# The first batch's key loads issued by ScalarE instead of SyncE

## The chip, the cores and the metric

One core of a Trainium2 chip runs the whole program in one launch. The metric is the device time of one execution in microseconds (us). It is the median of several runs, and lower is better. Every time below comes from the kernel's measured runs or from one profiled execution of it. The engines are called by the names that the profile gives them: PE (TensorE, matrix multiply), DVE (VectorE), ACT (ScalarE), POOL (GpSimd) and SP (SyncE, which only issues loads and stores here).

## The reference

Two stages follow each other. The first is attention of eight heads over a sequence of 576, for eight batches; the first four heads see a local window of 32 positions, the other four every 32nd position. The second is a mixture of four experts, each a causal attention on the first stage's output, of which two are taken for each token.

```python
def _attn_ref(q, k, v):                 # q, k, v: (8, 8, 576, 64)
    scores = scale * np.matmul(q, k.transpose(0, 1, 3, 2))
    ...
    mask_local = (rel >= 0) & (rel < stride)                  # stride = 32
    mask_strided = (rel >= 0) & (pos[None, :] % stride == pos[:, None] % stride)
    masks = np.stack([mask_local if h < H // 2 else mask_strided for h in range(H)], axis=0)
    ...
    return np.matmul(attn, v).astype(np.float32)

def _moe_ref(x, w_gate, wq, wk, wv, wo):
    ...
    for e in range(E):
        q = x @ wq[e]
        k = x @ wk[e]
        v = x @ wv[e]
        scores = scale * (q @ k.transpose(0, 2, 1))
        ...
        ye = a @ v @ wo[e]
        ...
            out += mask[..., None] * w[:, :, kk:kk + 1] * ye
```

## The kernel before

**Stages.** `stage1(b, hp)` does the first attention for one batch and one pair of heads; pairs 0 and 1 are local, pairs 2 and 3 strided. The second stage (`project`, `values2`, `attend`, `out_tile`) takes over when the four pairs of a batch are done. This case is about the opening, in which the four pairs of batch 0 are loaded, transposed and scored.

**What sets the order.** Every step is recorded by `op` (line 264) and issued by `schedule` (line 293) in the order of a hand-set list of numbers, `ORDER`. That one list gives the order on every engine: an instruction stands in its engine's queue where its step stands in the list, and each engine works through its queue in order. `FILL` puts matrix multiplies of no use (line 303, "fillers" below) ahead of some steps on PE.

**Batch 0's loads.** For a local pair, `load_qk` loads queries and keys with one DMA each, 288 KB (line 500, buffers `p_160` and `p_161` for pairs 0 and 1). For a strided pair it takes three DMAs each, of 18 rows of SBUF, 288 KB in all (line 505). Pair 2 goes to the buffer `nat_168` and pair 3 to `nat_172`; they are called **A** and **B** below. The value loads are at line 551, and the first loads of batch 1 at line 500 (`nat_176`).

**Counters.** The built program gives each load one of eight counters, `DMAHW0` to `DMAHW7`, in turn along the order in which it places the loads. A load that is to use a counter again is not issued before the earlier load on that counter has landed. The wait stands in the queue of the engine that issues the load.

**What follows a load.** For a local pair PE transposes the tiles (lines 573 and 586), ACT and DVE copy the results out of PSUM to `qkt` (line 340), and PE computes the scores from `qkt` (line 630). For a strided pair PE transposes `nat` (line 602), ACT and DVE copy (line 340) and PE scores (line 644). `qkt_180` serves pairs 0 and 2, `qkt_182` pairs 1 and 3.

Of the kernel before, what the change touches and what calls it, by code (L numbers as in the profile page):

```python
# [20 lines left out]
def attention_moe_kernel(  # L21
# [20 lines left out]
    nc = tc.nc  # L42
    B, H, S, D = q.shape
# [5 lines left out]
    NJ = S // STR  # L49
# [313 lines left out]
    for j in range(4):  # L363
        r = slice(32 * j, 32 * j + 32)
# [97 lines left out]
    def stage1(b, hp):  # L462
        batch[0] = b
        h0 = 2 * hp
# [4 lines left out]
        nat = (P2[3] if b == 0 and local else NAT).new(f"nat_{n}")  # L469
# [8 lines left out]
        def pair(x):  # L478
            return nat.t[:, x] if b == 0 else nat.t[:, x * S:(x + 1) * S]
# [10 lines left out]
        def raw(x):  # L490
            return nat.t[:, x * S:(x + 1) * S]

        def load_qk(src, x, h, y):
            base = src[b, h0 + h]
            if quad:
                p_ = 64 * h + 32 * y
                nc.sync.dma_start(raw(x)[p_:p_ + 32].rearrange("p (g d) -> p g d", d=32),
                                  base.rearrange("(g t) d -> t g d", t=32)[:, :, 32 * y:32 * y + 32])
            elif local:
                nc.sync.dma_start(pair(x), src[b, h0:h0 + 2].rearrange("h (p g) d -> (h p) (g d)", g=9))  # L500
            else:
                for r in range(3):
                    n_ = (11 if r < 2 else 10) * D
                    p_ = 64 * x + NJ * r
                    nc.sync.dma_start(nat.t[p_:p_ + NJ, :22 * D].rearrange("p (h c) -> p h c", h=2)[:, :, :n_], strips(base, 11 * r, n_))

        def strips(base, g0, n_):
            return bass.AP(tensor=base.tensor, offset=base.offset + g0 * D, ap=[[STR * D, NJ], [S * D, 2], [1, n_]])

        dm = [(0.51, 0.48)] if quad else [(0.44, 1.15)] if local else [(0.34, 0.67)] * 3  # L510
        for x, src in enumerate((q, k)):
            for h, y in ((0, 0), (0, 1), (1, 0), (1, 1)) if quad else ((0, 0),):
                op(*(("load_qk", {"SP": 0.54}, k0 - 30) if b > 1 else ("load_0", {"SP": 0.54}, first("x", b, hp))),
                   lambda e, src=src, x=x, h=h, y=y: load_qk(src, x, h, y), w=[nat[x]] if quad else [nat], dmas=dm)
# [8 lines left out]
        if quad:  # L523
            for x in range(2):
                op("tq", {"DVE": 0.66 if local else 1.11}, k0 - 13, lambda e, x=x: nc.vector.transpose(  # L525
                    turned(qkt.t, x), raw(x) if local else raw(x).rearrange("p (g d) -> p g d", d=32)),
                   r=[nat[x]], w=[qkt[x]])
            if not local:
                op("tq_out", {"ACT": 0.7, "POOL": 0.7}, k0 - 12, lambda e: (nc.scalar.copy if e == "ACT" else nc.gpsimd.tensor_copy)(
                    nat.t[:, :33 * NJ].rearrange("p (g r j) -> p g r j", g=11, r=3), thirds(qkt.t, 0)),  # L530
                   r=[qkt[0]], w=[nat[0], nat[1]])
# [29 lines left out]
        if local and not quad:  # L561
# [6 lines left out]
            for x in range(2):  # L568
# [7 lines left out]
                for a in range(2):  # L576
                    for h in range(2):
# [3 lines left out]
                           r=[tp], w=[qkt[0], qkt[1]])  # L581
# [7 lines left out]
            for h in range(2):  # L589
# [3 lines left out]
                   r=[tp], w=[qkt[0], qkt[1]])  # L593
# [25 lines left out]
        p = (PL if local else PSR).new(f"p1_{n}")  # L619
# [37 lines left out]
        for h in range(2):  # L657
            op("mask", {"DVE": dve(N // 2)}, k0 - 10, lambda e, h=h: nc.vector.tensor_tensor(
                pv()[:, h], sp[h].t[:, :ni * nk].rearrange("p (i c) -> p i c", c=nk), msk, ALU.add),
               r=[sp[h]], w=[p[h]])  # L660
# [23 lines left out]
        for step in range(6):  # L684
            for h_ in ((0, 2),) if step == 4 else groups:
                n_ = (h_[1] - h_[0]) * ni * nk
# [10 lines left out]
        if local:  # L697
            op("ptl", {"DVE": 0.73}, k0 - 2, lambda e: nc.vector.transpose(ptt.t[:, :640], p.t.rearrange("p h i c -> p (h i c)")),
               r=[p[0], p[1]], w=[ptt])
# [74 lines left out]
        for x, f_ in zip((xh, xl), XL4[b // 2]):  # L774
            c = slice(64 * (b % 2), 64 * (b % 2) + 64)
            op("xf", {"ACT": act(64), "POOL": 0.27}, k0 + 1.5, lambda e, x=x, f_=f_, c=c: (
                nc.scalar.copy if e == "ACT" else nc.gpsimd.tensor_copy)(f_.t[:, hp, c], f(x.t[:, S - 64:])),
               r=[x[3]] if local else [x[i] for i in range(3)], w=[f_[hp, b % 2]])
# [417 lines left out]
```

## Time and profile before

| | |
|---|---|
| Time, median of 3 runs | 443.27 us (443.09 to 443.4) |
| Profiled execution, its own time | 443.52 us |
| Its span (first to last instruction) | 441.8 us |
| PE busy in the span | 432.2 us, 98% |
| DVE, ACT, POOL busy | 360.0 (81%), 262.5 (59%), 218.5 us (49%) |
| DMA queues of loads and stores | one, SP's: 40.67 MB, 41.7% of 16 engines' time |

A row of the timeline gives the start in us from the span's start, the duration, the engine, the line, what is written and read, and the number of instructions merged in it. In brackets stands the idle time before it and what ended that. `SPq` is the queue in which SP issues DMAs: such a row is the issue, not the transfer.

### The profile page before, as it was taken

The page shows a single profiled execution, that of the slowest core. Times are in us where ns is not written, and L with a number is a line of the kernel's source. Part 1 is how long each engine was busy: PE and PEld are TensorE (multiplying, and loading weights), DVE is VectorE, ACT ScalarE, POOL GpSimd, SP SyncE. Part 2 cuts the span into 40 slices and gives each one's busy share as a digit, 9 for nine tenths or more (in the row PEclk, how much of TensorE's full clock was granted, in tenths as well). Part 3 has the DMA queues.
Part 4 walks back from the last instruction along what each step waited for, and adds up shares of the span by engine and source line. Part 5 has one row for each costly group of instructions (what it writes and reads, how often), then busy time and mean ns, then how long its engine had stood idle before and what let it go on. Part 6 is the DMA issues. An engine that isn't in the chain of part 4 may idle for free.

```text
span 441.8 us, 19136 instructions
## 1 busy us (share of the span) xinstructions
PE 432.2 (98%) x7762; PEld 384.8 (87%) x7762; DVE 360.0 (81%) x1133; ACT 262.5 (59%) x823; POOL 218.5 (49%) x404
## 2 busy tenths in 40 slices
PE   8999999999999999999999999999999999999996
PEld 8887998979799989989889888998789888988874
DVE  5798999999998999798898778788977985447761
ACT  2584635886656565647557555568684666354661
POOL 4263850786736445377336442747607472219430
PEclk9999999999999999999999999999999999999999
DMA  6666646656554635273446344074432120011013
GB/s 176 170 168 155 124 99 115 123 108 117 87 98 107 129 78 86 63 149 76 113 95 130 64 118 119 1 130 92 96 85 68 55 75 6 1 49 50 26 72 120
DMA packets 156272, 41.89 MB, mean 95 GB/s; under 512 B 145976, under 2 KB 149432, under 8 KB 156184
## 3 DMA queue, kind: packets, MB, share of 16 engines
q1 hardware_dynamic: 156184, 40.67, 41.7%
q8 instruction: 61, 1.00, 1.0%
q14 instruction: 27, 0.22, 0.2%
HBM read 31.20 MB, written 9.44 MB: 92 GB/s over the span
## 4 chain that ended last, share of the span: by engine, by line
PE 86%; DVE 9%; SPq 1%; DMA 1%; issue 1%; ACT 1%; POOL 0%; DVEq 0%; POOLq 0%; ACTq 0%
PE bank L908 20%; PE bank L1112 11%; PE bank L1083 11%; PE bank L855 9%; PE bank L994 7%; PE bank L1050 6%; PE bank L974 3%; PE bank L644 3%; PE bank L738 3%; PE bank L630 2%; PE bank L757 2%; PE bank L303 2%; DVE p L1001 1%; PE bank L818 1%; PE bank L920 1%; PE bank L708 1%
## 5 line engine op out<-in xcount | busy, mean ns | idle before, releaser
L1031 POOL TENSOR_SCALAR p<-p,st,wt 128x256 f32<-128x256 f32 (+3 forms) x128 | 77.2, 616 | 40.3 <-DVE st L1015 34.8
L1006 ACT ACTIVATE p<-p,st 128x512 f32<-128x512 f32 (+3 forms) x128 | 72.0, 568 | 9.1 <-DVE st L1001 9.0
L1001 DVE CUSTOM_DVE_ANT_0 p<-bank,m_cau 128x384 f32<-128x384 f32 (+3 forms) x128 | 58.8, 483 | 8.9 <-PE bank L994 7.5
L340 ACT COPY th<-bank 128x384 f32<-128x384 f32 (+2 forms) x106 | 41.8, 434 | 16.7 <-PE bank L1050 13.9
L525 DVE STREAM_TRANSPOSE qkt<-nat 128x576 f32<-128x576 f32 x48 | 47.6, 1004 | 1.7 <-DMA nat<-in_q_dram 1.2
L1083 PE MATMUL bank<-th,vs 128*64 128x192 f32 (+4 forms) x512 | 48.4, 337 | 0.1
L720 ACT CAST xh<-bank 128x160 fp32r<-128x160 f32 (+4 forms) x112 | 29.1, 320 | 29.1 <-PE bank L738 16.2
L929 ACT CAST qk<-bank 128x288 fp32r<-128x288 f32 x64 | 24.7, 400 | 35.9 <-PE bank L908 34.5
L1083 PEld LDWEIGHTS bank<-th,vs 128*64 128x64 f32 x512 | 33.7, 137 | 13.4 <-issue 6.2
L722 DVE TENSOR_TENSOR xl<-bank,xh 128x160 fp32r<-128x160 f32 (+4 forms) x112 | 32.2, 321 | 6.5 <-ACT xh L720 6.3
L855 PE MATMUL bank<-wh_v,xh 128*128 128x260 f32 x128 | 36.7, 287 | 0.0
L855 PE MATMUL bank<-wh_v,xl 128*128 128x260 f32 x128 | 36.2, 283 | 0.0
L855 PE MATMUL bank<-wl_v,xh 128*128 128x260 f32 x128 | 36.1, 282 | 0.0
L908 PE MATMUL bank<-xh,wh_q 128*128 128x288 f32 x120 | 35.8, 298 | 0.0
L908 PE MATMUL bank<-xh,wh_k 128*128 128x288 f32 x120 | 35.8, 298 | 0.0
L908 PE MATMUL bank<-xl,wh_q 128*128 128x288 f32 x120 | 35.4, 295 | 0.0
L908 PE MATMUL bank<-xl,wh_k 128*128 128x288 f32 x120 | 35.4, 295 | 0.0
L908 PE MATMUL bank<-xh,wl_q 128*128 128x288 f32 x120 | 35.3, 294 | 0.0
L908 PE MATMUL bank<-xh,wl_k 128*128 128x288 f32 x120 | 35.3, 294 | 0.0
L1050 PEld LDWEIGHTS bank<-ident,p 64*128 64x128 f32 x800 | 30.3, 139 | 4.7 <-issue 1.9
L1050 PE MATMUL bank<-ident,p 64*128 64x64 f32 x800 | 34.3, 226 | 0.0
L931 DVE TENSOR_TENSOR qkl<-bank,qk 128x288 fp32r<-128x288 f32 x64 | 27.6, 444 | 8.2 <-ACT qk L929 8.2
(183 smaller groups left out, 1269.2 us busy)
## 6 DMA issues: line engine op xcount, KB each, us to landing
out_dram<-ys SPq DMA_DIRECT2D x32, 256.0 KB
nat<-in_q_dram SPq DMA_DIRECT2D x96, 72.0 KB
nat<-in_k_dram SPq DMA_DIRECT2D x96, 72.0 KB
v<-in_v_dram SPq DMA_DIRECT2D x96, 40.0 KB
v<-in_v_dram SPq DMA_DIRECT2D x48, 54.0 KB
v<-in_v_dram SPq DMA_DIRECT2D x32, 48.0 KB
v<-in_v_dram SPq DMA_DIRECT2D x32, 45.0 KB
out_dram<-ys SPq DMA_DIRECT2D x8, 128.0 KB
```

Of the source, the lines that this page charges most:

```text
L340: (nc.scalar.copy if e == "ACT" else nc.vector.tensor_copy)(dst, src)
L525: op("tq", {"DVE": 0.66 if local else 1.11}, k0 - 13, lambda e, x=x: nc.vector.transpose(turned(qkt.t, x), raw(x) if local else raw(x).rea ...
L722: op("xl", {"DVE": dve(n_)}, key + 0.5, lambda e, s_=s_, x_=x_: nc.vector.tensor_sub(x_(xl.t), s_(xa.t), x_(f(xh.t))), r=[xa, xh[u]], w=[x ...
L855: nc.tensor.matmul(vp.t[:, :NV], xx.t[:, t0:t0 + 128], ww.t[:, kt, :], start=i == 0, stop=i == 11)
L908: nc.tensor.matmul(pj.t[:, :HS], ww.t[:, kt, ep * 128:(ep + 1) * 128], xx.t[:, c], start=i == 0, stop=i == 11)
L994: nc.tensor.matmul(sp[a].t[:, :nk], x.t[r, 0, q0:q0 + 128], y.t[r, 1, :nk], start=i == 0, stop=i == 2)
L1001: lambda e, sp=sp, p=p, a=a, nk=nk, ci=ci: nc.vector.tensor_tensor_reduce(out=p.t[:, a, :nk], in0=sp[a].t[:, :nk], in1=m_cau[:, S - nk:], ...
L1006: op("exp2", {"ACT": 0.285 + 0.00084 * nk}, k_ + 1, lambda e, p=p, a=a, ci=ci, nk=nk: nc.scalar.activation(p.t[:, a, :nk], p.t[:, a, :nk], ...
L1031: lambda e, p=p, a=a, ci=ci, t=t, nk=nk: nc.gpsimd.tensor_scalar(p.t[:, a, :nk], p.t[:, a, :nk], st.t[:, 20 + ci + a:21 + ci + a], wt.t[:, ...
L1050: nc.tensor.transpose(tp[hf].t[:, 64 * c:64 * c + 64], src, ident[r, r])
L1083: nc.tensor.matmul(acc.t[o, c0:c0 + cn], vw, th[a].t[:, s0:s0 + cn], start=j == 0, stop=j == idx[-1], skip_group_check=True)
L1112: nc.tensor.matmul(yp.t[:, :DM], xx.t[:, c0:c0 + 128], ww.t[:, ep, :], start=i == 0, stop=i == 5)
```

## The change

One line is added to `load_qk`, and two of its three loads use it: for batch 0 and the keys (`x` is 1) they are issued from ACT's queue (`nc.scalar`), else from SP's as before. The third form, `quad`, is for batches from 2 on and is not touched.

```diff
         def load_qk(src, x, h, y):
             base = src[b, h0 + h]
+            dma = nc.scalar if b == 0 and x else nc.sync
             if quad:
...
             elif local:
-                nc.sync.dma_start(pair(x), src[b, h0:h0 + 2].rearrange("h (p g) d -> (h p) (g d)", g=9))
+                dma.dma_start(pair(x), src[b, h0:h0 + 2].rearrange("h (p g) d -> (h p) (g d)", g=9))
             else:
                 for r in range(3):
...
-                    nc.sync.dma_start(nat.t[p_:p_ + NJ, :22 * D].rearrange("p (h c) -> p h c", h=2)[:, :, :n_], strips(base, 11 * r, n_))
+                    dma.dma_start(nat.t[p_:p_ + NJ, :22 * D].rearrange("p (h c) -> p h c", h=2)[:, :, :n_], strips(base, 11 * r, n_))
```

Eight DMAs change their queue: one for each local pair and three for each strided pair. `ORDER` is the same. The following lists show two queues near the start; after each row stand the semaphores it waits for (`PE_49`, `DVE_49` and the like are the engines' own, the `DMAHW` ones the loads' counters). Line numbers after the change are one higher.

ACT before, its first instructions: the copies out of the transposes of pairs 0 (`qkt_180`) and 1 (`qkt_182`).

```order
L340 ACT_TABLE_LOAD
L340 COPY qkt_180<-bank_66 64x128 [waits PE_49]
L340 COPY qkt_180<-bank_65 64x64x4 [waits DVE_49]
L340 COPY qkt_180<-bank_67 64x64x4 [waits DVE_49,PE_49]
L340 COPY qkt_180<-bank_65 64x64x4
L340 COPY qkt_180<-bank_67 64x64x4
L340 COPY qkt_182<-bank_69 64x64x4 [waits PE_49]
L340 COPY qkt_182<-bank_68 64x64x4 [waits DVE_49]
```

ACT after, from its first copy on; the two local key loads (`p_160` and `p_161`) stand ahead of the table load.

```order
L340 COPY qkt_180<-bank_66 64x128 [waits PE_49]
L340 COPY qkt_180<-bank_65 64x64x4 [waits DVE_49]
L340 COPY qkt_180<-bank_67 64x64x4 [waits DVE_49,PE_49]
L340 COPY qkt_180<-bank_65 64x64x4
L506 DMA nat_168<-in_k_dram 18x2x704 [waits DMAHW5_49]
L506 DMA nat_168<-in_k_dram 18x2x704 [waits DMAHW6_49]
L506 DMA nat_168<-in_k_dram 18x2x640 [waits DMAHW7_49]
L340 COPY qkt_180<-bank_67 64x64x4
L506 DMA nat_172<-in_k_dram 18x2x704 [waits DMAHW0_49]
L506 DMA nat_172<-in_k_dram 18x2x704 [waits DMAHW1_49]
L506 DMA nat_172<-in_k_dram 18x2x640 [waits DMAHW2_49]
L340 COPY qkt_182<-bank_69 64x64x4 [waits PE_49]
```

A's three key loads stand between the fourth and the fifth copy of pair 0, and B's behind the fifth. In the built program A's wait for the second landing on counters 5, 6 and 7, and B's for the third on counters 0, 1 and 2.

SP before, from A's loads on (ahead of them: the four local loads, on counters 0 to 3, and the gate's weights, on 4).

```order
L505 DMA nat_168<-in_k_dram 18x2x704 [waits DVE_49]
L505 DMA nat_168<-in_k_dram 18x2x704
L505 DMA nat_168<-in_k_dram 18x2x640
L505 DMA nat_168<-in_q_dram 18x2x704 [waits DMAHW0_49]
L505 DMA nat_168<-in_q_dram 18x2x704 [waits DMAHW1_49]
L505 DMA nat_168<-in_q_dram 18x2x640 [waits DMAHW2_49]
L505 DMA nat_172<-in_q_dram 18x2x704 [waits DMAHW3_49,DVE_49]
L505 DMA nat_172<-in_q_dram 18x2x704 [waits DMAHW4_49]
L505 DMA nat_172<-in_q_dram 18x2x640 [waits DMAHW5_49]
L505 DMA nat_172<-in_k_dram 18x2x704 [waits DMAHW6_49]
L505 DMA nat_172<-in_k_dram 18x2x704 [waits DMAHW7_49]
L505 DMA nat_172<-in_k_dram 18x2x640 [waits DMAHW0_49]
```

SP after, from A's loads on (ahead of them: the two local query loads, on counters 1 and 3, and the gate's weights, on 4).

```order
L506 DMA nat_168<-in_q_dram 18x2x704 [waits DVE_49]
L506 DMA nat_168<-in_q_dram 18x2x704
L506 DMA nat_168<-in_q_dram 18x2x640
L506 DMA nat_172<-in_q_dram 18x2x704 [waits DMAHW0_49,DVE_49]
L506 DMA nat_172<-in_q_dram 18x2x704 [waits DMAHW1_49]
L506 DMA nat_172<-in_q_dram 18x2x640 [waits DMAHW2_49]
L552 DMA v_184<-in_v_dram 32x5x64 [waits DMAHW3_49]
L552 DMA v_184<-in_v_dram 32x5x64 [waits DMAHW4_49]
L552 DMA v_184<-in_v_dram 32x6x64 [waits DMAHW5_49]
L552 DMA v_184<-in_v_dram 32x5x64 [waits DMAHW6_49]
L501 DMA nat_176<-in_q_dram 128x576 [waits DMAHW7_49]
L501 DMA nat_176<-in_k_dram 128x576 [waits DMAHW0_49,DVE_49]
```

A's queries stand where A's keys stood, with the first use of counters 5, 6 and 7. Their second use is by the third and fourth value load and by the queries of batch 1, which before stood behind all strided loads. On PE, DVE and POOL no row moves.

## Rows read from the trace of the kernel before

**Rows 1.** The page: busy us of each engine (share of the span), number of instructions.

```profile
PE 432.2 (98%) x7762; PEld 384.8 (87%) x7762; DVE 360.0 (81%) x1133; ACT 262.5 (59%) x823; POOL 218.5 (49%) x404
```

**Rows 2.** Stretches: from:to, length, busy us as in rows 1, clock, DMA share, GB/s.

```profile
5.30:11.60 6.30, 6.30 (x53) 6.08 (x52) 2.94 (x16) 2.48 (x6) 0.85 (x4) 1.00 0.61 140
...
20.60:45.00 24.40, 22.94 (x709) 20.18 (x709) 22.28 (x59) 15.18 (x45) 12.02 (x16) 1.00 0.66 158
45.00:437.00 392.00, 389.17 (x6705) 346.88 (x6704) 324.40 (x1010) 237.96 (x760) 200.36 (x363) 1.00 0.40 86
```

**Rows 3.** Waits of PE, first 60 us: who <- for whom, us in total, times, longest.

```profile
PE bank L303 <- POOL ident masks.py:199: 1.4, 1, 1.4
PE bank L602 <- DVE xl L722: 0.7, 1, 0.7
```

**Rows 4.** Timeline of SP's queue of issues, opening; start us, duration us.

```profile
3.14 1.12 SPq L505 DMA_DIRECT2D nat<-in_k_dram  x3
...
8.77 0.27 SPq L505 DMA_DIRECT2D nat<-in_q_dram  x1
9.19 0.27 SPq L505 DMA_DIRECT2D nat<-in_k_dram  x1
9.79 0.27 SPq L505 DMA_DIRECT2D nat<-in_k_dram  x1
10.77 0.27 SPq L505 DMA_DIRECT2D nat<-in_k_dram  x1
11.81 0.32 SPq L551 DMA_DIRECT2D v<-in_v_dram  x1
...
12.96 1.20 SPq L551 DMA_DIRECT2D v<-in_v_dram  x1
14.21 0.44 SPq L551 DMA_DIRECT2D v<-in_v_dram  x1
```

**Rows 5.** Waits of SP's queue, first 16 us.

```profile
SPq L505 <- DMA nat<-in_k_dram: 0.8, 2, 0.5
```

**Rows 6.** Timeline of ACT, opening.

```profile
8.43 0.83 ACT L340 COPY qkt<-bank 64x128 f32<-64x128 f32 x2 [6.35 <-PE bank L586]
...
10.69 0.42 ACT L340 COPY qkt<-bank 64x256 f32<-64x256 f32 x1
11.13 0.42 ACT L340 COPY qkt<-bank 64x256 f32<-64x256 f32 x1
11.99 1.58 ACT L340 COPY qkt<-bank 64x256 f32<-64x256 f32 x4 [0.44 <-DVE qkt L340]
14.84 0.76 ACT L340 COPY qkt<-bank 128x324 f32<-128x324 f32 x2 [1.26 <-PE bank L602]
```

**Rows 7.** Timeline of PE, opening; line 303 is the fillers.

```profile
10.88 0.83 PE L303 MATMUL bank<-ident 128*128 128x128 f32 x6
11.64 1.04 PE L630 MATMUL bank<-qkt 64*32 64x64 f32 x80
12.61 1.60 PE L303 MATMUL bank<-ident 128*128 128x128 f32 x12
14.14 0.95 PE L602 MATMUL bank<-ident,nat 54*128 54x54 f32 x24
...
15.86 0.92 PE L644 MATMUL bank<-qkt 64*64 64x54 f32 x48
```

**Rows 8.** DMA issues of the first 60 us: number of them, KB each.

```profile
v<-in_v_dram SPq DMA_DIRECT2D x24, 40.0 KB
...
nat<-in_q_dram SPq DMA_DIRECT2D x2, 288.0 KB
```

**Rows 9.** Table of stretches again: the last column is what the DMA moved, GB/s.

```profile
7.50:12.00 4.50, 4.50 (x75) 4.38 (x75) 2.96 (x7) 2.48 (x7) 0.00 (x0) 1.00 0.60 142
...
15.60:20.00 4.40, 4.27 (x141) 3.75 (x142) 3.90 (x10) 2.30 (x6) 0.72 (x1) 1.00 0.87 241
```

**Rows 10.** Timeline of PE, its first instructions.

```profile
1.42 1.65 PE L303 MATMUL bank<-ident 128*128 128x128 f32 x6 [1.42 <-POOL ident masks.py:199]
```

## Prediction

> **What bounds the kernel now.** The first view is the page's busy line: TensorE (PE) is busy for 432.2 of 441.8 us [rows 1]. The second is the table of stretches: PE is busy for all 6.30 us from 5.3 to 11.6, for 22.94 of 24.40 us from 20.6 to 45, and for 389.17 of 392 us after that [rows 2]. The third is PE's own waits in the first 60 us: 1.4 us at the very start for the identity matrix, 0.7 us once for VectorE, and no load at all [rows 3]. So a load that comes earlier frees nothing on PE, and whatever holds PE in the opening moves everything behind it.
>
> The opening is then read engine by engine. On SP's queue, the issue times also tell landings, since an issue that waits for a counter starts when the load on it lands: A's three key loads go out from 3.14, and SP's issues at 8.77, 9.19 and 9.79 are the ones that wait for them [rows 4]; the wait view has two of SP's waits as ended by landing keys [rows 5]. On ScalarE (ACT), the last copy of the first pair's transposed keys and queries starts at 10.69 and takes 0.42; the copies of the second pair follow at 11.13 and 11.99, and those of A's transposes at 14.84 [rows 6]. On PE, fillers start at 10.88, the first scores at 11.64, twelve fillers at 12.61, A's transposes at 14.14 and A's scores at 15.86 [rows 7]. The first scores need ACT's copy of 10.69, which ends at 11.11: 0.53 us before PE gets there. That is the only cover PE has against a late ACT.
>
> **What the change removes and adds.** SP loses eight issues. Their price is small (1.12 us for the three from 3.14 on, 0.27 each for those around 9 [rows 4]), and since PE waits for no load the gain is nothing. The two local key loads move to the head of ACT's queue, where ACT has nothing to do before 8.43 but load a table [rows 6]; they cost nothing, since the table load is done long before that.
>
> The six strided key loads are the matter. In ACT's instructions they stand where the written order has them, between the copies: A's three after the fourth copy, before the one of 10.69, and B's three right behind it. And each waits: A's for the second landing on counters 5, 6 and 7, B's for the third on counters 0, 1 and 2. I work out when these come.
>
> SP's queue now has A's queries where A's keys were, so they land when the keys did, at 8.77, 9.19 and 9.79, and B's queries where A's queries were: 10.77, 11.81 and about 12.0 [rows 4]. The second users of counters 5, 6 and 7 are the third and fourth value load and the queries of batch 1. The third value load can go out at 8.77 and takes 1.20 us to issue, the next 0.44, if they take what they took at 12.96 and 14.21 [rows 4]; so the queries of batch 1 go out near 10.5. They land behind B's queries (12.0), four value loads (some 40 KB each, 164,000 bytes) and their own 288 KB (295,000 bytes) [rows 8]. The DMA moved 241 GB/s in a stretch of such loads and 142 in one of strided loads [rows 9], so the value loads take 0.7 us and the queries 1.2: they land at **13.9**. The bounds: if everything from 9.79 on, B's queries too (295,000 bytes, 754,000 in all), went at 241, it would be 12.9; if at 142, 15.1.
>
> So A's last key load is issued at 13.9 instead of before 4.26. It takes about 0.35 (no row of before has ACT issue a load; the nearest are SP's, 0.27 to 0.44), the held copy 0.42 and its signal a few hundredths: the first scores start at 14.75, not 11.64. **First term: +3.1 us** (bounds +2.1 and +4.3).
>
> Next, B's keys wait for the other load of batch 1 and two value loads, which land 1.2 and twice 0.2 us behind the 13.9: 15.5. ACT has issued the last one at 15.8, makes the five copies of the second pair (0.42 each [rows 6]) by 17.9, and is then due for A's transposes, which on PE's moved schedule end at about 18.2. So this second hold is covered by 0.3 us; if the first cover were gone it would cost what it lacks, up to a microsecond where B's keys come late.
>
> A's keys themselves must be there when PE reaches A's transposes, 14.14 + 3.1 = 17.25. Issued at 13.9, they share the DMA with the other load of batch 1 and four value loads (295,000 and 164,000 bytes, 1.9 us at 241) and need 2.1 us of their own at 142: 17.9 if they go last, 16 if the two queues take turns from the start. I take the middle of nothing and 0.6. **Second term: +0.3 us** (0 to +0.6, and to +1.6 with the second hold uncovered).
>
> What goes back later: PE's idle time from 20.6 to 45 is 1.46 us [rows 2], and the one long wait in it is for VectorE [rows 3], whose work comes from PE's and ACT's and moves along. I take nothing, with -1.2 as the bound. SP's own later loads wait for PE's progress and have run ahead by then, so they add nothing. Sum: **+3.4 us**, bounds about +1 and +6.
>
> [...] The trace shows the opening's loads limited by what the DMA moves: three strided loads of 288 KB in all issued within 1.2 us land 5 to 6 us later [rows 4]. [...]
>
> **The rivals.** *The held issue does not hold the copies.* Were a waiting load to let later copies pass, the first scores would be on time, and only A's transposes would wait for keys landing at 16 to 17.9 instead of being due at 14.14: +1.9 to +3.8, 445.2 to 447.1 us. Against it: on SP the loads behind a waiting one stay behind it, up to 1.0 us between 9.79 and 10.77 [rows 4]. Chance 0.04.
>
> *PE's clock falls.* PE would stand idle for about 3 us, which it never does in this trace after 1.4. [...] Chance 0.13; it decides if the first scores come later than my 14.75 rather than sooner.
>
> *Faster.* SP is free of eight issues, its loads of batch 1 go out up to 4 us earlier, and VectorE's chain behind them gets ahead: at most the 1.2 us of waits PE has there, 442.1 us. It decides only if the counters that ACT waits for are filled before the copy of 10.69 is due, that is if batch 1's queries land by then, 3 us before my estimate and at the time they are issued. Chance 0.03.
>
> *Nothing happens.* The hold stays within PE's 0.53 us of cover: 443.3 us. It needs those queries by 10.9. The same rows speak against it. Chance 0.04.
>
> **How the numbers follow.** The profiled execution took 443.52 us around its span of 441.8, 0.25 above the median of three, 443.27. 443.52 + 3.4 = 446.9; against the median, which later runs are compared with, **446.7 us**. Forecast (+1.3 to +4.9): 0.76. Range for 8 in 10: from 444.8, the low bound of the first term with a little given back, to 449.0, which takes in the clock's case. A difference under 0.2% (0.9 us) can't be told from none here. Faster 0.03, the same 0.05 (the case of nothing and the edge of the forecast), slower 0.92.
>
> **What would show it.** In the profile after: ACT's copy of 10.69 near 14.3, with idle time before it that a DMA ends; three loads of nat from in_k issued by ACT near 13 to 14 and three more to about 15.8; PE's first scores near 14.75 with idle time before them, released by ACT; A's transposes at about 17.5, and from there to the end a constant shift. SP's loads of batch 1 go out near 10.5 instead of behind the issue at 14.21. If the first scores stand within 0.5 us of 11.64, my reading of ACT's queue is wrong; if they stand near 14.75 and the end moves by much less, PE had time to give back that I have not seen; if fillers show 1.6 us per dozen more, the clock fell.

## The result and the profile after

The changed kernel takes **447.45 us** (median of 4 runs, 446.57 to 450.92) against 443.18 for the kernel before beside it. The ratio is 1.011, 95% interval 1.0072 to 1.0148: 3.2 to 6.6 us slower. Six later runs gave 448.3 us, ratio 1.0112 (1.0083 to 1.0141). Two single executions that took far longer than all others (795.17 us of the kernel before, 658.96 of one experiment) are left out of the ratios. The profiled execution is the slowest of the first four: 450.92 us around a span of 449.2, with a mean granted clock of 0.989; the other three had 0.995 to 0.998. So its opening is read for what happens where, and the medians for what it costs.

PE's busy line of the page, which answers to [rows 1]: 5.5 us more for the same number of instructions.

```profile
PE 437.7 (97%) x7762; PEld 389.2 (87%) x7762; DVE 359.5 (80%) x1133; ACT 262.1 (58%) x823; POOL 217.7 (48%) x404
```

The table of stretches (as [rows 2]; the last three columns are granted clock, DMA share, GB/s). The clock is below 1.00 from 11.6 to 45 (0.79 and 0.87 on the mean) and 1.00 again behind. About 4.7 of PE's 5.5 us lie in the products from 16.25 to 27.1, which took 12.1 us by their rows, against 7.4 for the same ones before; the column falls to 0.50 there.

```profile
11.60:20.60 9.00, 6.18 (x124) 5.33 (x123) 2.49 (x7) 2.80 (x8) 0.72 (x1) 0.79 0.62 156
20.60:45.00 24.40, 23.62 (x655) 20.90 (x657) 20.41 (x54) 15.31 (x42) 10.75 (x15) 0.87 0.47 122
45.00:437.00 392.00, 389.24 (x6887) 347.13 (x6884) 327.90 (x1020) 238.42 (x763) 201.60 (x365) 1.00 0.41 87
```

Cut finer, one microsecond each, the same trace shows 1.00 still while PE stands idle, and 0.50 from 17, shortly after it works again, to about 27.

```profile
14.00:15.00 1.00, 0.00 (x0) 0.00 (x0) 0.00 (x0) 0.16 (x1) 0.00 (x0) 1.00 0.71 160
...
17.00:18.00 1.00, 1.00 (x6) 1.00 (x6) 0.45 (x1) 0.99 (x3) 0.40 (x1) 0.50 0.62 132
...
26.00:27.00 1.00, 1.00 (x6) 0.86 (x5) 1.00 (x4) 0.40 (x2) 0.00 (x0) 0.50 0.00 0
```

PE's waits in the first 60 us (as [rows 3]): a new one, for ACT, at the first scores.

```profile
PE bank L631 <- ACT qkt L340: 2.7, 1, 2.7
```

ACT's timeline (as [rows 6]; `ACTq` rows are ACT's issues of loads). The fourth copy ends at 11.33, then nothing until pair 2's keys (A) go out at 13.53; the held copy runs at 14.84; pair 3's keys (B) and the five copies of the second pair follow, and then ACT waits for PE.

```profile
10.47 0.86 ACT L340 COPY qkt<-bank 64x256 f32<-64x256 f32 x2 [0.56 <-DVE qkt L340]
13.53 1.27 ACTq L506 DMA_DIRECT2D nat<-in_k_dram  x3
14.84 0.41 ACT L340 COPY qkt<-bank 64x256 f32<-64x256 f32 x1 [3.51 <-DMA nat<-in_k_dram]
15.45 1.03 ACTq L506 DMA_DIRECT2D nat<-in_k_dram  x3
16.52 1.99 ACT L340 COPY qkt<-bank 64x256 f32<-64x256 f32 x5 [1.27 <-PE bank L631]
20.00 0.43 ACT L340 COPY qkt<-bank 128x324 f32<-128x324 f32 x1 [1.49 <-PE bank L603]
```

The chain of waits through that place names the load that ACT waited for first: a value load, issued on SP, which landed at 13.51. Behind it come the three issues of A's keys, the held copy and, at 15.30, the scores.

```profile
9.00 4.51 DMA v<-in_v_dram
...
13.53 0.58 ACTq L506
...
14.15 0.28 ACTq L506
...
14.47 0.33 ACTq L506
...
14.84 0.42 ACT qkt L340
...
15.30 1.02 PE bank L631 x63
```

PE's timeline (as [rows 7]): two score products go out at 12.29, since they need only the earlier copies; the other 78 wait until 15.30. The twelve fillers behind them took 2.41 us instead of 1.60, A's transposes start at 18.60 instead of 14.14, and A's scores take 1.54 instead of 0.92.

```profile
12.29 0.30 PE L631 MATMUL bank<-qkt 64*32 64x64 f32 x2
15.30 1.02 PE L631 MATMUL bank<-qkt 64*32 64x64 f32 x78 [2.72 <-ACT qkt L340]
16.25 2.41 PE L303 MATMUL bank<-ident 128*128 128x128 f32 x12
18.60 1.95 PE L603 MATMUL bank<-ident,nat 54*128 54x54 f32 x24
...
21.63 1.54 PE L645 MATMUL bank<-qkt 64*64 64x54 f32 x48
...
27.60 1.04 PE L631 MATMUL bank<-qkt 64*32 64x64 f32 x80
```

SP's queue (as [rows 4]): the first loads of batch 1 go out at 10.73, four microseconds sooner than the 14.69 of before, which frees nothing on PE.

```profile
8.05 2.10 SPq L552 DMA_DIRECT2D v<-in_v_dram  x4
10.73 0.35 SPq L501 DMA_DIRECT2D nat<-in_q_dram  x1
```

### The profile page after: what moved, and what is told of

It reads as the page before. It is cut to its first block, busy times and chain, and to the rows that moved or that the text cites. A ratio compares the mean times of both kernels' runs of the same rounds, so it can differ in the third digit from the quotient of the medians.

```text
span 449.2 us, 19136 instructions
## 1 busy us (share of the span) xinstructions
PE 437.7 (97%) x7762; PEld 389.2 (87%) x7762; DVE 359.5 (80%) x1133; ACT 262.1 (58%) x823; POOL 217.7 (48%) x404
## 4 chain that ended last, share of the span: by engine, by line
PE 82%; DVE 8%; DMA 4%; SPq 3%; issue 1%; ACT 1%; ACTq 0%; DVEq 0%
PE bank L909 20%; PE bank L1113 10%; PE bank L1084 10%; PE bank L856 9%; PE bank L995 7%; PE bank L1051 6%; PE bank L975 3%; PE bank L739 3%; PE bank L645 3%; PE bank L631 2%; DMA v<-in_v_dram 2%; SPq L498 2%; PE bank L758 2%; PE bank L303 2%; PE bank L819 1%; DMA nat<-in_q_dram 1%
## 5 line engine op out<-in xcount | busy, mean ns | idle before, releaser
L340 ACT COPY th<-bank 128x384 f32<-128x384 f32 (+2 forms) x106 | 41.8, 436 | 16.5 <-PE bank L1051 13.9
```

The lines of the kernel that those rows point to most:

```text
L340: (nc.scalar.copy if e == "ACT" else nc.vector.tensor_copy)(dst, src)
```

## The experiments

The theory after the result: the loss is ACT, held ahead of a copy that PE needs, then A's keys, which are issued late, and then the lower clock (0.50) that follows PE's idle time. The rivals: the second queue costs by itself (transfers that share the DMA), or the clock has no part in it. The microseconds behind a ratio are its distance from 1 times 443.2.

**The hold without a load.** The kernel before with copies of no use on ACT at the place in question.

```diff
         def load_qk(src, x, h, y):
+            if b == 0 and hp == 2 and x:
+                for _ in range(6):
+                    nc.scalar.copy(idle, m_cau[:, :512])
```

> The kernel before with all loads on SP, and six copies of a constant (128x512) on ACT between its fourth and fifth copy, where the change put the three key loads of pair 2. They should take some 0.6 us each, so hold ACT about 3.6 us. Theory (the loss is ACT held ahead of that copy, and PE's clock falling in the idle time): first scores at 14.5 to 15.3 instead of 11.64, a stretch at the lower clock behind them, and a time of 446.3 to 449, like the changed kernel's 447.45. Rival 1 (the loss is in the transfers: two queues share the DMA, or keys land late): no load has moved, so 443.3 to 444. Rival 2 (the hold alone, the clock falls by chance): 446.3 with the granted clock at 1.000.

Measured: 447.05 us, ratio 1.0087 (1.0072 to 1.0102), +3.9 us. ACT's timeline shows the hold, PE's the wait:

```profile
11.78 3.88 ACT L497 COPY idle<-m_cau 128x512 f32<-128x512 f32 x6
15.67 2.44 ACT L340 COPY qkt<-bank 64x256 f32<-64x256 f32 x6
```

```profile
16.13 1.02 PE L634 MATMUL bank<-qkt 64*32 64x64 f32 x78 [3.12 <-ACT qkt L340]
17.08 2.38 PE L303 MATMUL bank<-ident 128*128 128x128 f32 x12
```

The scores came later than expected (16.13 instead of 14.5 to 15.3), since PE's own start-up took a microsecond longer in this execution; the wait is the one foreseen. No load moved, and most of the loss is there, lower clock included (0.71 in the stretch from 15.6 to 20.6, 0.994 to 0.996 on the mean in all five runs). The transfers are not needed to explain that part.

**Half the hold.** The same with `range(3)`.

> The kernel before with three instead of six copies of a constant on ACT at the same place: six held ACT for 3.9 us, so three should hold it for 1.9, and PE idle for some 1.4. Theory (the hold less its cover is what PE loses, and the clock falls only in the longer idle time): 444.4 to 445.0, the clock at 1.000 in the opening. Rival (the loss is in proportion to the hold, cover or not): half of the 3.85 us that six copies cost, 445.1 and more. Rival (any idle time of PE brings the lower clock): 445.5 or more with a stretch at 0.5.

Measured: 443.88 us, ratio 1.0021 (1.0 to 1.0041), +0.9 us. PE waits 1.16 us, and the clock stays up:

```profile
12.91 1.02 PE L634 MATMUL bank<-qkt 64*32 64x64 f32 x78 [1.16 <-ACT qkt L340]
```

```profile
15.60:20.60 5.00, 4.86 (x112) 4.24 (x108) 4.05 (x10) 2.69 (x7) 1.06 (x2) 1.00 0.82 227
```

Half a microsecond under what was expected, and far from half of 3.9: the price is the hold less its cover, and behind this shorter idle time the clock stayed up in all twelve runs (0.999 or 1.000 on the mean).

**Three loads instead of eight.** Only pair 2's keys on ACT, at their written place.

```diff
-            dma = nc.scalar if b == 0 and x else nc.sync
+            dma = nc.scalar if b == 0 and x and hp == 2 else nc.sync
```

> Only pair 2's three key loads on ACT, at the same place between the copies; the local ones and pair 3's on SP. Fewer loads are moved, but the ones that ACT waits for now (the first queries of batch 1 and two value loads) stand behind pair 3's keys on SP, about 2 us later than in the changed kernel. Theory: the hold is longer, first scores near 16.3, time 447.5 to 451, slower than the whole change. Rival (the loss grows with the number of loads moved or with both queues sharing the DMA): three of eight loads, 444.5 to 446.

Measured: 448.99 us, ratio 1.013 (1.0111 to 1.0148), +5.8 us. Three loads cost at least as much as eight, as the landing that ACT waits for demands: it is now ended by queries, the last of the three issues ends at 16.81, and PE waits 4.9 us.

```profile
15.32 1.49 ACTq L506 DMA_DIRECT2D nat<-in_k_dram  x3
16.86 2.42 ACT L340 COPY qkt<-bank 64x256 f32<-64x256 f32 x6 [5.73 <-DMA nat<-in_q_dram]
```

**The same three loads, elsewhere in ACT's queue.** The condition is the same (`hp == 2`), and step 88 (pair 2's keys) is moved ahead of ACT's copies in `ORDER`.

```diff
-        0, 2, 1, 3, 4, 45, 13, 6, 44, ...
+        0, 2, 1, 3, 4, 45, 88, 13, 6, 44, ...
```

> The same three loads on ACT as in the run with pair 2 alone, but written ahead of ACT's first copy, where they wait only for the memset of the buffer and the second load's landing. Theory (place and wait, not queue): ACT is free again near 5.5, the first scores at 11.6, clock 1.000, 442.8 to 443.8, no difference from before. Rival (a second queue costs by itself, by sharing the DMA): 444.5 or more. Rival (earlier keys help): under 442.3.

Measured: 442.67 us, ratio 0.9988 (0.9972 to 1.0004). The same loads on the same queue cost nothing: the place and the wait that comes with it are the cause, not the queue. ACT has issued them by 4.69, and the first scores stand at 11.35.

```profile
2.79 1.90 ACTq L506 DMA_DIRECT2D nat<-in_k_dram  x3
4.71 1.28 ACT L340 ACT_TABLE_LOAD   x1 [4.71 <-DMA p<-in_q_dram]
```

The profiled execution, at 443.76 us one of the slower of the twelve, also has a stretch at the lower clock, far behind the opening and behind a wait of only 1.02 us for a value load:

```profile
64.97 1.37 PE L739 MATMUL bank<-pt,v 32*64 32x32 f32 x82 [1.02 <-DMA v<-in_v_dram]
```

```profile
67.00:68.00 1.00, 1.00 (x52) 0.83 (x38) 0.63 (x3) 0.14 (x1) 0.00 (x0) 0.50 0.74 153
```

**The second hold alone.** Only pair 3's keys on ACT (`hp == 3`).

> Only pair 3's three key loads on ACT, at their place behind the fifth copy. They wait for two value loads and the first queries of batch 1, as pair 2's did in the run with those alone, where the hold ended near 16.8. Theory: the first scores are on time (11.6), ACT makes the second pair's copies from about 16.8 on and those of pair 2's transposes only near 19, so pair 2's scores start near 20 instead of 15.86: 446.5 to 448.5. Rival (the second hold is covered, as the prediction had it for the whole change): 443.0 to 444.0.

Measured: 448.42 us, ratio 1.011 (1.0081 to 1.0139), +4.9 us. The first scores were on time (11.74). ACT was held to 17.58, and A's scores, which need copies queued behind, came at 20.37:

```profile
13.47 4.07 ACTq L506 DMA_DIRECT2D nat<-in_k_dram  x3
17.58 3.15 ACT L340 COPY qkt<-bank 64x256 f32<-64x256 f32 x8 [6.37 <-DMA nat<-in_k_dram]
```

```profile
20.37 1.54 PE L645 MATMUL bank<-qkt 64*64 64x54 f32 x48 [4.53 <-ACT qkt L340]
```

In the whole change this hold is hidden behind the first: there ACT idles 1.49 us behind the five copies, waiting for PE. Alone it costs as much as everything together, but alone it is also longer: the last of pair 3's issues ended at 17.54, against 16.48 in the whole change.

**The local keys alone.** Only the two local loads on ACT (`b == 0 and x and local`).

> Only the two local key loads on ACT; they stand at the head of its queue. Theory (they wait for nothing and nothing stands behind them): 442.8 to 443.6, as before, first scores at 11 to 12.3. Rival (a second queue costs by itself): 444.5 or more. Rival (an earlier start of the loads helps): under 442.3.

Measured: 443.26 us, ratio 0.9999 (0.9974 to 1.0024). No loss and no gain; the first scores came at 12.76, later than expected, behind a start-up of PE a microsecond longer than in the kernel before's trace.

**The clock, with more fillers.** The changed kernel, with `FILL` ahead of the first scores raised from 3 to 13.

> The changed kernel with ten more filler products of PE ahead of the first scores (about 0.26 us each, 2.6 us), so that PE works through most of the time in which ACT is held. Theory (hold and clock both): the hold stays, the first scores start near 15, but the clock does not fall: 445.5 to 446.5 with the granted clock at 1.000, a gain of 1 to 2 us on the changed kernel. Rival (the clock has no share, all is hold and late keys): 447 to 448, as the changed kernel. Rival (PE's idle time is given back later and only the clock costs): 443.5 to 444.5.

Measured: 448.64 us, ratio 1.012 (1.0104 to 1.0137), +5.3 us: a miss. The clock stayed up (1.000 in three of four runs, 0.999 in the profiled one), and yet it is no faster. The waits of PE in the whole trace show the rest of the hold, a wait for A's keys, and 1.3 us at one place put down to issue, far behind the opening:

```profile
PE bank L631 <- ACT qkt L340: 1.5, 1, 1.5
...
PE bank L645 <- issue: 1.3, 1, 1.3
PE bank L603 <- DMA nat<-in_k_dram: 0.7, 1, 0.7
```

**The busy ACT with the same fillers.** The six copies and 13 fillers.

> The kernel before with the six copies on ACT and ten more fillers on PE ahead of the first scores: the same hold, no load moved and so no late key, and PE idle for less than a microsecond. Theory (the clock's fall costs where no late load hides it): no stretch at the lower clock in the opening, pair 2's scores about 1.3 us sooner than with the hold alone, 445.6 to 446.3 against 447.05. Rival (the clock's share is nothing, as the changed kernel with fillers would suggest, which was no faster): 446.7 to 447.4.

Measured: 448.34 us, ratio 1.0108 (1.008 to 1.0136): a miss again. The opening went as expected, with A's scores 1.6 us sooner than in the run with the hold alone (19.98 against 21.60); the time did not follow. Two of the six runs had a clock of 0.996, so ten fillers do not always keep it up, and issue waits stand out once more:

```profile
PE bank L761 <- issue: 1.1, 1, 1.1
PE bank L648 <- issue: 1.0, 1, 1.0
```

**The same cover with no instruction more.** The changed kernel with its three fillers there made four times as wide.

```diff
                 for _ in range(o.fill):
-                    nc.tensor.matmul(bank[:, :128], ident, ident, start=True, stop=True)
+                    if i == 18:
+                        nc.tensor.matmul(bank[:, :512], ident, m_cau[:, :512], start=True, stop=True)
+                    else:
+                        nc.tensor.matmul(bank[:, :128], ident, ident, start=True, stop=True)
```

> The changed kernel in which the three fillers ahead of the first scores are four times as wide (512 columns instead of 128), so that PE is busy some 2.4 us longer there with no instruction more. With ten more fillers the opening's clock stayed at 1.000 and yet the kernel was no faster; its trace had 1.5 us of waits of PE put down to issue, those without added instructions mostly 0.2 to 0.8. Theory (the clock's fall costs 1 to 3 us, and the ten instructions cost it back): no stretch at the lower clock in the opening, first scores near 15.3, issue waits under 1 us, 445.3 to 447.0. Rival (the clock's share is nothing, or fillers cost by themselves): 447.5 to 449.

Measured: 446.73 us, ratio 1.0069 (1.0043 to 1.0095), +3.1 us, as the theory had it. In the profiled execution the clock was 1.00 throughout the opening, and no wait of PE is put down to issue. So the clock's fall does cost, 0.7 to 1.6 us by the medians (447.45 and 448.3 against 446.73), though the intervals of the ratios overlap a little. The wide fillers do not always keep it up: four of the twelve runs had a mean clock of 0.992 to 0.996. These took 447.83 to 450.18 us, the other eight (0.998 to 1.000) 444.68 to 447.14, so within this one kernel the runs with the lower clock are all slower. PE's timeline also gives the hold and the late keys at the full clock:

```profile
11.29 2.74 PE L304 MATMUL bank<-m_cau,ident 128*128 128x512 f32 x6
...
15.44 1.02 PE L634 MATMUL bank<-qkt 64*32 64x64 f32 x78 [1.19 <-ACT qkt L343]
...
18.89 0.92 PE L606 MATMUL bank<-ident,nat 54*128 54x54 f32 x23 [0.70 <-DMA nat<-in_k_dram]
...
24.16 1.04 PE L634 MATMUL bank<-qkt 64*32 64x64 f32 x80
```

That the ten instructions themselves cost the time back in the other two kernels is only argued: two traces with issue waits of 1.5 and 2.7 us in all, against 0 to 1.1 in the others; but the trace of half the hold, which has no added product on PE, has 1.7, and in the narrow-filler kernel three runs at a clock of 1.000 still took 448.37 to 448.94.

**The change once more.**

> The changed kernel once more, on the same chip and beside the other runs of this call. Theory (ACT held until batch 1's queries land, then pair 2's keys late): first scores again near 15.3, pair 2's transposes not before 18.5, at whatever moment PE's own start-up ends, since both are set by landings; 447 to 448.5, the granted clock between 0.995 and 0.999. Rival (the landings wander from run to run by a microsecond or more): first scores under 14.5 or over 16.

Measured: 448.3 us (446.38 to 449.74, 6 runs), with clocks of 0.989 to 0.996, lower than expected. The scores came at 15.98, a hair short of the 16 from which the rival would have held: ACT's first issue went out at 14.21 instead of 13.53, so the landings do wander by some 0.7 us. A's keys wander more: PE's transposes waited for them until 20.76, against 18.72 and 18.89 with the narrow and the wide fillers. The lower clock was there again:

```profile
15.98 1.39 PE L631 MATMUL bank<-qkt 64*32 64x64 f32 x78 [4.54 <-ACT qkt L340]
...
20.76 1.49 PE L603 MATMUL bank<-ident,nat 54*128 54x54 f32 x23 [0.25 <-DMA nat<-in_k_dram]
```

```profile
15.60:20.60 5.00, 4.53 (x91) 3.96 (x91) 0.98 (x2) 2.27 (x6) 0.72 (x1) 0.50 0.59 114
```

Over the ten runs of the changed kernel the time goes with the clock: the six with a mean of 0.994 to 0.998 took 446.38 to 447.66 us, the four with 0.989 to 0.992 took 449.02 to 450.92. The kernel before has such executions too, but fewer: eight of the 68 that ran beside the experiments had a mean of 0.991 to 0.996 and took 443.34 to 446.76 us, the other sixty, at 0.998 to 1.000, 441.56 to 444.51.

**Two tries at something faster.** First the kernel before without the three fillers ahead of the first transposes; then this and, beside it, the local and pair 2's keys on ACT ahead of its copies.

> The kernel before without the three fillers ahead of the first transposes (0.83 us of PE at the upper clock). In all traces PE's start-up shifted the opening as a whole by what its own first products took, so PE, not the loads, set the pace there. Theory: first transposes 0.8 us sooner, the loads still in time, 442.2 to 442.8. Rival (the first loads, which landed at 4 to 8 us, become the bound, or the clock rises later): 442.9 to 443.6.

> The local keys and pair 2's keys on ACT, ahead of its copies, pair 3's on SP, and the three fillers ahead of the first transposes left out. Theory: ACT waits for nothing late, loads land a little sooner, PE starts 0.8 us sooner: 441.8 to 442.7, a little faster than before. Rival (no load was late, so the place of the loads adds nothing to the trimmed start): the same as the kernel before trimmed in the same way, within 0.3.

Measured: 442.46 us (ratio 0.9987, 0.9955 to 1.0018) and 443.33 us (0.9997, 0.9972 to 1.0022). Neither differs from before by more than the measurement can tell, and the second missed its range. In the second PE got going 0.7 us sooner and then waited 0.7 for VectorE at 17.80; six of its twelve runs had a clock of 0.991 to 0.996. In its trace the lower clock follows two waits of 0.34 and 0.55 us, the second of them this:

```profile
40.40 0.54 PE L603 MATMUL bank<-ident,nat 54*128 54x54 f32 x11 [0.55 <-DVE xl L723]
```

```profile
43.00:44.00 1.00, 1.00 (x48) 1.00 (x46) 0.85 (x3) 0.24 (x1) 0.00 (x0) 0.50 0.59 133
```

No version tried beats the kernel before.

## Why the prediction was right, and where not

The time (446.7 forecast, 447.45 and 448.3 measured) and the main mechanism were right. The make-up of the sum was not, and the second measurement lies 1.6 us above the forecast.

- **PE waited for no load before, so earlier loads bring nothing**: right. Local keys alone, or pair 2's keys ahead of the copies, change nothing.
- **ACT is held between its fourth and fifth copy until loads on reused counters land**: right, and shown from three sides: a hold without loads costs most of it (3.9 us), the same loads at another place cost nothing, and fewer loads with a later landing cost no less.
- **First term, +3.1**: somewhat small. The last of A's three issues started at 14.47 in the profiled execution, half a microsecond behind the estimate of 13.9 and inside its bounds. The value loads were under-estimated: by the working all four would have landed 0.7 us behind 12.0, but the one that ACT waited for first landed at 13.51 (14.19 when the change ran again). Batch 1's queries, where a chain of waits shows them (narrow fillers), landed at 14.40. The scores stood at 15.30 and 15.98 in the two traces of the change, and at 15.23 and 15.44 with narrow and wide fillers, instead of 14.75: +3.6 to +4.3 on 11.64. Since the landing sets that moment, PE's own start-up no longer matters for it.
- **The second hold is covered by the first**: right, and the run with pair 3 alone shows what a somewhat longer one costs uncovered, 4.5 us of PE's time.
- **Second term, +0.3**: too small. With the wide fillers, as with the narrow ones, PE stands 0.7 us in the middle of A's transposes for a key load. Hold and late keys together shift the second batch of scores by 4.7 us there (24.16 against 19.46, the start-up's 0.4 included), not by 3.4.
- **PE's clock**: the step that failed. The forecast left its fall to a rival with a chance of 0.13; it fell in both traces of the changed kernel and was below 1.000 on the mean in all ten runs. The 1.6 us more per dozen fillers by which the forecast would tell the fall, and which the clock's case in its range took in, no run shows for the dozen behind the first scores: it took 0.81 more than the 1.60 of before in the first trace (2.41) and 1.33 in the second (2.93). Two half dozens wholly at 0.50 took 1.65 each, 0.71 more than before. By the second batch of scores the profiled execution is 8.1 us behind before (27.60 against 19.46), the wide fillers' 4.7 (24.16): 3.4 us of that execution are the clock. In most others it took less, and part of the slow products only filled the wait for A's keys: in the profiled execution the slow fillers ended at 18.66, about when the keys came in with the wide ones.
- **Nothing goes back later**: not quite. With the clock up the opening loses 4.7 us, and the time 3.1. Two traces, of before and of the wide fillers, can be followed: 4.7 us apart at the second batch of scores, 4.0 at the first product of the projections (line 908; 45.95 against 49.96), 2.4 at the end of the span (441.8 against 444.2). Most of the last step is chance in a single trace: the kernel before has one wait of PE far behind the opening, ended at 365.15, which the others lack:

```profile
PE bank L757 <- DVE st L1001: 1.4, 1, 1.4
```

So the errors ran against each other: the hold and the keys were about a microsecond too small, the clock was left out, and what goes back later, 0.7 us by 46 us in these two traces, was left out too. The number was better than its working. Why 0.7 us goes back is not settled, nor whether it does in other executions, nor is the cost of added filler instructions. Taking away only the counters' wait while the loads stay where they are in ACT's queue was not tried.

## What to carry to other kernels

Before moving a load to another engine's queue, read what stands behind it there and which landing it will wait for; here the earlier loads brought nothing (443.26 us with the local keys alone, 442.67 with pair 2's ahead), while ACT's copies behind a waiting issue were held (3.51 us idle before the one at 14.84). If a load is to go to a computing engine, put it ahead of that engine's work, where its wait has cover: the same three loads took the kernel to 448.99 us between the copies and to 442.67 ahead of them. When TensorE gets a new idle time, look at the granted clock behind it as well, and weigh it by the mean clock of all runs, not by one profile.

## What was not expected of the hardware

The granted clock stayed at 1.00 in traces where PE's new idle time ahead of the first scores was 1.2 or 1.5 us, and was at 0.50 behind new idle times of 2.7 to 4.9 us. The length of one idle time does not settle it, though: it was at 0.50 behind a wait of 1.02 us (pair 2's keys ahead) and behind waits of 0.34 and 0.55 us (the last kernel tried), while the kernel before kept 1.00 behind its wait of 1.4. What else decides, the runs here do not show. In the profiled execution of the change the clock was still 1.00 while PE stood idle and fell only after PE was at work again at 15.30 (0.93 from 16 to 17, 0.50 from 17 on); when the change ran again it fell while PE stood idle (0.78 from 14 to 15, 0.50 from 15 to 16).

PE's start-up varies from execution to execution of the same opening: the ten products of its warm-up took 3.05 to 4.47 us in the traces here, which moves everything that PE, and not a landing, sets. In it single products took 634 ns at first and 380 later, and the first six fillers 1.65 us against 0.83 later. The clock column reads 1.00 in every microsecond up to 7 in the traces of before and after, so what makes these first products slow, the runs here do not show.
